# New order tables for a gated recurrent-attention and GeGLU kernel, and an earlier load of its guard flag

## The chip, the cores and the metric

One NeuronCore of a Trainium2 chip runs the kernel alone. Five engines work side by side: TensorE (PE, matmuls; the loading of its weights is shown as PEld), VectorE (DVE), ScalarE (ACT), GpSimd (POOL) and SyncE (SP), which here issues nearly all transfers. Each has its own queue of instructions and works through it in order; semaphores tie the queues together. The metric is the device time of one execution in microseconds.

## The reference

The input `x` (2048 x 448) is layer-normed. One branch is a recurrent attention in four segments of 512 positions with 16 heads of 28: causal softmax attention inside each segment, mixed with a read from a memory that the earlier segments have written. The other branch is a GeGLU feed-forward net of width 1792. The result is `x + s * silu(ffn)`.

```python
for s in range(N):                       # N = 4 segments
    logits = einsum(qs, ks) * scale + mask
    a_dot = softmax(logits) @ vs
    pq = phi(qs)                         # phi(t) = t + 1 if t > 0 else exp(t)
    a_mem = (pq @ M) / (pq @ z + 1e-06)
    o = g * a_mem + (1 - g) * a_dot      # g = sigmoid(beta)
    pk = phi(ks)
    M = M + pk^T @ vs
    z = z + sum(pk)
...
xn = layernorm(x)
s = attention(xn) @ wo
g = silu((gelu(xn @ w_gate) * (xn @ w_up)) @ w_down)
return x + s * g
```

## The kernel before

`fast_path` computes everything with all weights held in SBUF. It takes the softmax without a running maximum, which is allowed as long as the logits stay small. `guard` works out from the weights' norms whether they do, and leaves a 0 or 1 in the one-element tile `oki`. At the end every engine loads that flag into a register (`load_ok`, L1264) and branches on it (`tc.If`, L1679): with 1 the program is over, with 0 the slow `general_path` is run after it. The branch jumps over the code of `general_path`.

The work is cut into some 1170 named operations, each an `Op` with the engines that may run it, its length and latency, what it depends on, and which buffers it takes or uses. For segment `s`:

- `sc{s}{k}` are the ten steps of scores (L984), `ex{s}{k}{0,1}` their exponentials on ACT (L999, 128 x 1024 each), `mk` the causal masks on POOL (L1010), `pv` the products with the values (L1046), `ou` the copy of the sums out of PSUM (L882).
- `wq`, `wk`, `wv{s}{n}` are the projections (L713; two `full` units of three matmuls, then a `visit` `wr...` with the two half-height ones), `ev...` their evictions, `tq`, `tk`, `tr` DMA transposes on SP.
- `exwk`, `exwq` (L825), `mi` (L830) and `ph` (L838, L843) make phi; `up` (L859) adds to the memory, `rd{s}{g}` on PE (L897) reads it; `den`, `dc`, `rd{s}{side}{j}` and `rb` are transfers that invert and broadcast the denominators, `sm` and `ca` (L908, L952) multiply by them, and `cb` (L955) sums both sides into the single buffer `oT`.
- `gu` and `gh` (L1088, L1103) are the gate and up projections, `ge` the gelu on ACT (L1113), `hm` the product on DVE (L1118); `dn{s}{b}{k}` is the down projection of a block of 128 rows in groups of up to five matmuls (L1148), `th` and `sg` its silu, `wo{s}{b}` the output projection (L1173), `fm` and `fa` (L1178, L1164) the closing product and sum, `st` the store. The last block (L1192 to L1222, `last_block`) is cut into three column pieces `330`, `331`, `332`; the last store, `st332`, is issued by ACT, all others by SP.

`arrange` puts all operations into one list. It keeps a clock for each engine, counts for each operation the length and latency written at its definition, and takes, of what could start soonest (within `AHEAD`), the operation with the lowest `prio`. `PRIO` overrides the priority of each operation by name; `STEP` says behind which step of the scores a piece of PE work, or a phi of segment 2, may come. The list that comes out is then issued in this order, and each engine's queue keeps it. So the lengths and the tables shape the program that is built, and nothing else: at run time the engines go by their queues and semaphores.

The four stages of feed-forward and attention follow one another as `ORDER` says: G0, A0, A1, G1, A2, G2, A3, G3, and the last down projections. In A0 to A3 the PE fills the time between score steps with projections of the next segments, down projections and memory reads. Scores of the first two segments go through three pairs of PSUM banks, those of the others through two. The loads of `wo_sb` (four pieces), of `x_sb` for segments 2 and 3 and of the two halves of `wd_sb` are issued by SP among the transposes towards the end of G0; the first `dn` group of a block reads only the first half of `wd_sb`.

Of the kernel before, what the change touches and what calls it, by code (L numbers as in the profile page):

```python
# [53 lines left out]
class Buf:  # L54
# [284 lines left out]
def fast_path(tc, A_x, A_wq, A_wk, A_wv, A_wo, A_beta, B_w_gate, B_w_up, B_w_down, out):  # L339
# [19 lines left out]
    with ExitStack() as ctx:  # L359
# [89 lines left out]
        def act(name, n, fn, func=None, **kw):  # L449
            return op(name, {"ACT": (n / 1200 + 0.05, n / 1200 + 0.165)}, fn, act=func, **kw)  # L450

        def dve(name, t, fn, **kw):
            return op(name, {"DVE": (t, t + 0.085)}, fn, **kw)
# [1259 lines left out]
```

## Time and profile before

| | |
|---|---|
| median of 3 runs | 231.68 us (231.41 to 234.36) |
| the profiled execution | 232.09 us |
| its span, first to last instruction | 230.3 us |
| granted TensorE clock, mean | 0.996 |
| DMA over the span | 25.12 MB, mean 109 GB/s |

The profile is of one execution. Its times are counted from the span's start; what lies around the span is 1.8 us. A row of the windows gives a stretch, its length, then for PE, PEld, DVE, ACT and POOL the busy time and the number of instructions, then the granted PE clock (1.00 is full), the mean busy share of the DMA engines and the GB/s that they moved. A row of the timeline gives the start, the length, the engine, the line, the operation with its tiles, and in brackets how long the engine had been idle before and what released it. Rows of one line (L1264, L1679) give the shortest, median and longest duration in ns, and the first and last start. An engine with a q behind its name (ACTq, SPq) stands for its sequencer: transfers issued, loads of registers, branches, semaphores.

### The profile page before, as it was taken

How to read it: one execution, taken by the hardware profiler on the slowest of the kernel's cores; microseconds unless marked ns; L12 is line 12 of the kernel's file. 1: busy time of each engine (PE TensorE's matmuls, PEld its weight loads, DVE VectorE, ACT ScalarE, POOL GpSimd, SP SyncE). 2: the span in 40 equal slices, each digit the busy share in tenths (PEclk: the TensorE clock that was granted, in tenths of full speed). 3: DMA queues.
4: the chain of work that ended last, by engine and by line, in shares of the span. 5: the costliest groups of instructions: out<-in, count | busy, mean ns of one | idle time of the engine just before them, and what ended most of it. 6: DMA issues, size and time to landing. Idle time of an engine off the chain costs nothing.

```text
span 230.3 us, 4484 instructions
## 1 busy us (share of the span) xinstructions
PE 220.0 (96%) x1571; PEld 96.0 (42%) x1571; DVE 153.7 (67%) x291; ACT 152.0 (66%) x211; POOL 129.4 (56%) x222
## 2 busy tenths in 40 slices
PE   7999999889999999999999999999999999999980
PEld 3544443333544434344444444444444434444560
DVE  3799998868955795773865686873646445457381
ACT  4799636999898779333788879433788874323120
POOL 8501400679488699504599989671198488406200
PEclk9999999999999999999999999999999999999998
DMA  7999369954336882317702232273400037152011
GB/s 213 274 364 223 70 149 252 248 113 90 32 76 72 201 99 59 89 43 194 184 25 65 41 76 65 55 191 89 93 1 6 10 83 188 39 142 55 5 58 31
DMA packets 44710, 25.12 MB, mean 109 GB/s; under 512 B 30808, under 2 KB 40856, under 8 KB 44680
## 3 DMA queue, kind: packets, MB, share of 16 engines
q1 hardware_dynamic: 43704, 24.05, 45.8%
q10 hardware_dynamic: 976, 0.71, 1.0%
q8 instruction: 14, 0.23, 0.4%
q14 instruction: 16, 0.13, 0.2%
HBM read 16.00 MB, written 2.98 MB: 82 GB/s over the span
## 4 chain that ended last, share of the span: by engine, by line
PE 74%; ACT 8%; DVE 6%; DMA 5%; issue 2%; SPq 1%; ACTq 0%; DVEq 0%
PE pp L1088 13%; PE ps L1088 13%; PE ps L1148 13%; PE ps L713 10%; ACT pt L999 6%; PE ps L1173 4%; PE pp L984 4%; PE ps L1046 3%; PE pp L1103 3%; PE ps L1103 3%; DMA rb<-rdr 2%; PE ps L571 2%; DMA rdr<-dc 2%; DMA qT<-e 2%; PE pp L1148 2%
## 5 line engine op out<-in xcount | busy, mean ns | idle before, releaser
L999 ACT ACTIVATE pt<-pp 128x1024 bf16<-128x1024 f32 x75 | 73.3, 1037 | 12.2 <-PE pp L984 10.2
L1010 POOL TENSOR_SCALAR_AFFINE_SELECT pt<-pt 128x256 bf16<-128x256 bf16 x128 | 53.8, 444 | 26.0 <-ACT pt L999 23.4
L1148 PE MATMUL ps<-wd_sb,hT 128*128 128x448 bf16 x182 | 39.2, 354 | 0.5 <-DVE qs L749 0.4
L1113 ACT ACTIVATE gl<-pp 128x512 bf16<-128x512 f32 x28 | 15.8, 595 | 29.1 <-PE pp L1103 23.3
L1148 PEld LDWEIGHTS <-hT 128*128 128x128 bf16 x210 | 18.8, 98 | 20.6 <-issue 5.5
L1118 DVE TENSOR_TENSOR hT<-gl,pp 128x512 bf16<-128x512 bf16 x28 | 18.4, 681 | 11.5 <-ACT gl L1113 11.5
L1118 DVE TENSOR_TENSOR hT<-gl,ps 128x512 bf16<-128x512 bf16 x28 | 18.7, 677 | 10.9 <-ACT gl L1113 8.4
L1113 ACT ACTIVATE gl<-ps 128x512 bf16<-128x512 f32 x28 | 16.6, 597 | 13.1 <-PE ps L1088 6.7
L1088 PEld LDWEIGHTS <-wu_sb 128*128 128x128 bf16 x168 | 16.4, 98 | 20.0 <-issue 0.3
L1088 PEld LDWEIGHTS <-wg_sb 128*128 128x128 bf16 x168 | 14.9, 98 | 22.5 <-issue 7.2
L908 POOL TENSOR_TENSOR om<-om,rb 128x512 f32<-128x512 f32 x12 | 14.9, 1269 | 16.2 <-DMA rb<-rdr 16.2
L713 PEld LDWEIGHTS <-xnT 128*128 128x128 bf16 (+1 forms) x192 | 15.0, 97 | 20.6 <-issue 10.1
L1088 PE MATMUL ps<-xnT,wg_sb 128*128 128x512 bf16 x84 | 22.8, 380 | 0.0
L955 POOL TENSOR_TENSOR oT<-oa,om 128x512 bf16<-128x512 f32 x12 | 15.9, 1334 | 12.3 <-DVE oa L952 12.3
L1088 PE MATMUL pp<-xnT,wg_sb 128*128 128x512 bf16 x84 | 22.8, 380 | 0.0
L1088 PE MATMUL ps<-xnT,wu_sb 128*128 128x512 bf16 x84 | 22.7, 379 | 0.1
L1088 PE MATMUL pp<-xnT,wu_sb 128*128 128x512 bf16 x84 | 22.7, 379 | 0.0
L1164 POOL TENSOR_TENSOR oo<-sg,x_sb 128x448 bf16<-128x448 f32 (+1 forms) x13 | 12.9, 995 | 12.7 <-DVE sg L1215 10.1
L984 PE MATMUL pp<-qT,kT 32*128 32x512 bf16 (+3 forms) x238 | 17.3, 301 | 1.9 <-ACT pt L999 1.8
L830 POOL TENSOR_SCALAR e<-e 128x896 bf16<-128x896 bf16 (+1 forms) x12 | 12.8, 1068 | 10.9 <-ACT e L825 10.9
L645 POOL TENSOR_TENSOR rs<-rs,nhalf 128x1 f32<-128x1 f32 (+1 forms) x7 | 6.1, 883 | 16.5 <-DVE rs L640 16.5
L882 DVE COPY oa<-ps 128x512 f32<-128x512 f32 x16 | 10.9, 683 | 5.8 <-PE ps L1046 5.5
(119 smaller groups left out, 327.1 us busy)
## 6 DMA issues: line engine op xcount, KB each, us to landing
rb<-rdr SPq DMA_DIRECT2D x28, 256.0 KB
out_dram<-oo SPq DMA_DIRECT2D x15, 112.0 KB
wd_sb<-in_B_w_down_dram SPq DMA_DIRECT2D x2, 784.0 KB
x_sb<-in_A_x_dram SPq DMA_DIRECT2D x3, 448.0 KB
rdr<-dc SPq DMA_DIRECT2D x28, 32.0 KB
wg_sb<-in_B_w_gate_dram SPq DMA_DIRECT2D x2, 384.0 KB
wu_sb<-in_B_w_up_dram SPq DMA_DIRECT2D x2, 384.0 KB
wg_sb<-in_B_w_gate_dram SPq DMA_DIRECT2D x1, 576.0 KB
```

Source lines behind the costliest of these rows:

```text
L713: nc.tensor.matmul(out=self.bank.ap()[:, 0:D], lhsT=self.xT.ap()[r, c, n * P:(n + 1) * P], rhs=self.w[r, c, :], **kw)
L908: oU[s, g, 1] = t, gps(f"sm{s}{g}", 1.22, lambda t=t, r=r: nc.gpsimd.tensor_tensor(out=t.ap(), in0=t.ap(), in1=r.ap(), op=ALU.mult), deps= ...
L955: oT[s][1].append(gps(f"cb{s}{g}", 1.22, lambda g=g, t=t, tm=tm: nc.gpsimd.tensor_tensor(out=dst.ap()[:, g, :], in0=t.ap(), in1=tm.ap(), o ...
L984: nc.tensor.matmul(out=S2[i // 2].ap(i % 2)[:, c0:c0 + n], lhsT=kT[s][0].ap()[r, g, kb * P:(kb + 1) * P], rhs=qT[s][0].ap()[r, g, kb * P:L ...
L999: nc.scalar.activation(out=dst, in_=src, func=ACT.Exp, scale=scale)
L1010: nc.gpsimd.affine_select(out=v, in_=v, pattern=[[0, 2], [1, P]], compare_op=ALU.is_ge, fill=0.0, base=0, channel_multiplier=-1)
L1088: nc.tensor.matmul(out=bf[fc].ap(i), lhsT=w[:, c, fc * P:(fc + 1) * P], rhs=xT.ap()[:, c, :], start=begins and c == 0, stop=not begins and ...
L1103: nc.tensor.matmul(out=bf[fc].ap(i), lhsT=wh_sb[r, fc * P:(fc + 1) * P], rhs=xT.ap()[r, NC3, :], start=fc in begins, stop=fc in ends)
L1113: a = act(f"ge{s}{fc}", L, lambda: nc.scalar.activation(out=gl.ap(), in_=bf[fc].ap(0), func=ACT.Gelu_apprx_tanh), func="gelu", deps=[o], a ...
L1118: nc.vector.tensor_tensor(out=hT[s][0].ap()[:, fc, :], in0=gl.ap(), in1=bf[fc].ap(1), op=ALU.mult), deps=[a] + held,
L1148: nc.tensor.matmul(out=bank.ap()[:, 0:D], lhsT=hT[s][0].ap()[:, fc, b * P:(b + 1) * P], rhs=wd_sb[:, fc, :], start=(fc == 0), stop=(fc == ...
L1164: o = op(f"fa{s}{b}{h}", eng, lambda: (nc.vector if o.on == "DVE" else nc.gpsimd).tensor_tensor(out=oo.ap()[:, r], in0=t.ap()[:, r], in1=x ...
```

## The change

All entries of `PRIO` and most of `STEP` have new values; the operations that they order are the same. Five lengths at the operations' definitions are changed: the latency of an ACT and of a DVE operation, the power on POOL in the layer norm (`pw`), phi of the queries on DVE, and the exponentials of the scores. The flag's load is issued as soon as `th332` and `m332`, the last tanh and the last product of the closing block, have been issued, in place of after everything; and its value's bounds check is left out.

```diff
 PRIO = {
-    "ag00": -1122.63, "ag01": -1135.403, "ag10": -834.064, "ag11": -1044.988, "ag12": -837.494,
...
+    "ag00": -89.052, "ag01": -89.062, "ag10": -262.926, "ag11": -262.956, "ag12": -89.072,
...
 }
 STEP = {
-    "dn000": 9, "dn0010": 10, "dn005": 2, "dn010": 3, "dn0110": 7, "dn015": 6, "dn020": 3,
...
+    "dn000": 10, "dn0010": 3, "dn005": 6, "dn010": 0, "dn0110": 4, "dn015": 2, "dn020": 1,
...
 }
@@
         def act(name, n, fn, func=None, **kw):
-            return op(name, {"ACT": (n / 1200 + 0.05, n / 1200 + 0.165)}, fn, act=func, **kw)
+            return op(name, {"ACT": (n / 1200 + 0.05, n / 1200 + 0.18)}, fn, act=func, **kw)
 
         def dve(name, t, fn, **kw):
-            return op(name, {"DVE": (t, t + 0.085)}, fn, **kw)
+            return op(name, {"DVE": (t, t + 0.09)}, fn, **kw)
@@
-                o = gps(f"pw{s}{bs[0]}", 0.56, lambda r=r: nc.gpsimd.tensor_tensor(
+                o = gps(f"pw{s}{bs[0]}", 0.61, lambda r=r: nc.gpsimd.tensor_tensor(
@@
-                pqT[s][1].append(dve(f"ph{nm}{s}{half}", 1.47, lambda:
+                pqT[s][1].append(dve(f"ph{nm}{s}{half}", 1.35, lambda:
@@
-                    x = act(f"ex{s}{k}{pr}", 2 * L, ex, func="exp", deps=[o],
+                    x = act(f"ex{s}{k}{pr}", 2 * L + 24, ex, func="exp", deps=[o],
@@
         def load_ok():
-            got["ok"] = nc.values_load(oki[0:1, 0:1], min_val=0, max_val=1)
+            got["ok"] = nc.values_load(oki[0:1, 0:1], min_val=0, max_val=1,
+                                       skip_runtime_bounds_check_because="it is the least of comparisons")
@@
         with tc.manual_schedule():
+            closing = {f"th{LAST}{NB - 1}2", f"m{LAST}{NB - 1}2"}
             for o in arrange(ops):
                 if o.fn is not None:
                     o.fn()
-            load_ok()
+                closing.discard(o.name)
+                if not closing and "ok" not in got:
+                    load_ok()
```

The two programs have the same number of instructions on PE and DVE. The orders that they give each engine, where the prediction goes into them, read as follows (score steps marked with ^, visits with ~):

```
PE, start of A0, before: sc00^ wk10 wk11 wr1wk0~ wk13 wk12 wr1wk2~ sc01^ sc02^ wq11 wq10 wr1wq0~ sc03^ dn010 sc04^
PE, start of A0, after:  sc00^ wk10 wk11 wr1wk0~ sc01^ wq10 dn010 wq11 wr1wq0~ sc02^ dn015 sc03^ wv10 dn0110 wv11 wr1wv0~ sc04^
SP, before: tr10 tr13 wo_in0 x2 tr11 tr12 wo_in3 wd_in0 wo_in2 wo_in1 x3 wd_in1
SP, after:  tr10 tr13 wo_in0 wo_in3 wo_in2 wo_in1 x2 tr11 tr12 wd_in1 wd_in0 x3
ACT, A0, before: ex011 ex020 ex021 ... ex051 exwk10 ex060 ex061 exwk11 ex070 ... ex081 exwq11 ex090 ex091 exwq10 ex100
ACT, A0, after:  ex011 exwk10 ex020 ex021 ... ex090 ex091 exwk11 ex100 ex101 exwq10 ex110 ex111 exwq11
DVE, end of G2, before: hm212 ca21 hm213 ca22 ca20 ca23 evwv30 evwv31
DVE, end of G2, after:  hm212 hm213 ca20 ca21 fm11 evwv30 evwv31
PE, start of A3, after: sc30^ dn210 wo11 dn230 dn235 sc31^ dn2310 wv30 wv31 wr3wv0~
PE, end, before: dn3010 dn325 dn3210 wo33 wo32 dn330a dn335a dn3310a dn330b ... dn3310c
PE, end, after:  dn330a dn300 ... dn305 dn3010 wo30 wo33 dn335a dn3310a dn330b ... dn3310c
DVE, end, before: m330 y330 fa330 m331 y331 m332 y332 fa332 load
DVE, end, after:  m330 y330 m331 y331 m332 load y332 fa332   (fa330 on POOL)
ACT, end, before: th332 st332 load branch
ACT, end, after:  th332 load st332 branch
SP, end, before: st330 st331 load check branch
SP, end, after:  st330 load st331 branch
```

356 rows, old and new, of tables (PRIO, STEP) are left out of this document.

## The prediction

> **What bounds the kernel now.** I read the page first (busy shares, the slices, the chain of waits), then the windows, one stretch per stage, then the timeline of the two places where TensorE (PE) stands, and last the lines of the closing branch.
>
> ```profile
> PE 220.0 (96%) x1571; PEld 96.0 (42%) x1571; DVE 153.7 (67%) x291; ACT 152.0 (66%) x211; POOL 129.4 (56%) x222
> PE   7999999889999999999999999999999999999980
> PE 74%; ACT 8%; DVE 6%; DMA 5%; issue 2%; SPq 1%; ACTq 0%; DVEq 0%
> ```
>
> PE is at work in 220.0 of the span's 230.3 us, and 74% of the chain that ended last is PE. The other engines are each busy about two thirds of the time, so they matter only where one of them makes PE wait. The windows say where that is (first column the stretch, then its length and PE's busy time in it; DVE, ACT and POOL follow).
>
> ```profile
> 1.26:16.40 15.14, 15.01 (x91) 7.21 (x93) 10.82 (x32) 11.79 (x26) 7.46 (x27) 1.00 1.01 302
> 16.40:39.00 22.60, 22.54 (x120) 8.93 (x114) 21.18 (x51) 14.95 (x25) 3.66 (x3) 1.00 0.84 177
> 39.00:52.00 13.00, 11.15 (x94) 4.54 (x90) 9.61 (x25) 12.46 (x17) 8.04 (x19) 1.00 0.94 185
> 52.00:64.00 12.00, 11.88 (x120) 5.31 (x120) 10.73 (x18) 10.90 (x14) 8.37 (x17) 1.00 0.40 59
> 64.00:140.00 76.00, 76.00 (x602) 32.75 (x600) 51.29 (x82) 56.27 (x71) 56.56 (x91) 1.00 0.44 93
> 140.00:162.00 22.00, 22.00 (x126) 9.07 (x124) 13.75 (x21) 10.74 (x17) 12.47 (x12) 1.00 0.41 112
> 162.00:187.00 25.00, 24.55 (x204) 10.30 (x204) 15.12 (x26) 20.72 (x24) 16.95 (x33) 1.00 0.10 23
> 187.00:217.80 30.80, 30.76 (x176) 13.52 (x176) 15.07 (x25) 11.69 (x18) 14.80 (x16) 1.00 0.35 90
> 217.80:225.60 7.80, 6.08 (x60) 4.38 (x58) 5.88 (x15) 2.51 (x6) 0.49 (x1) 1.00 0.16 52
> 225.60:230.30 4.70, 0.00 (x0) 0.00 (x0) 0.00 (x0) 0.00 (x0) 0.00 (x0) 0.79 0.12 29
> ```
>
> Between 1.26 and 217.8 PE is idle for 0.13 + 0.06 + 1.85 + 0.12 + 0.00 + 0.00 + 0.45 + 0.04 = 2.65 us, and 1.85 of that is the start of the first attention (39 to 52), where ACT is busy 12.46 of 13.00. The end has 1.72 us more (217.8 to 225.6) and 4.70 us with no work on any engine. Both programs hold the same instructions on PE, so a new order can save PE time only out of these idle stretches. That caps what can be won: 2.65 us in the middle, plus what the closing part gives. 2% of 231.68 is 4.6 us, about what a measurement of this kernel can tell from no change.
>
> **The tail: the guard's load.** The rows are the load of `oki` (L1264) on three engines, the branch that tests it and what follows it (L1679), and the last instructions.
>
> ```profile
> L1264 DVEq TENSOR_LOAD <-oki x1: 541/541/541, 225.3 to 225.3; - x1
> L1264 ACTq TENSOR_LOAD <-oki x1: 479/479/479, 226.0 to 226.0; - x1
> L1679 DVEq COMPARE_BRANCH  x1: 72/72/72, 226.0 to 226.0; - x1
> L1679 ACTq COMPARE_BRANCH  x1: 58/58/58, 226.6 to 226.6; - x1
> L1679 DVEq EVENT_SEMAPHORE  x1: 21/21/21, 228.9 to 228.9; - x1
> L1679 ACTq EVENT_SEMAPHORE  x1: 17/17/17, 229.3 to 229.3; - x1
> 224.47 0.25 DVE L1212 TENSOR_TENSOR sg<-sg,ps 128x96 f32<-128x96 f32 x1
> 224.75 0.25 ACT L1209 ACTIVATE th<-ps 128x96 f32<-128x96 f32 x1 [1.12 <-DVE sg L1212]
> 225.03 0.26 DVE L1215 SCALAR_TENSOR_TENSOR sg<-th,sg 128x96 f32<-128x96 f32 x1 [0.32 <-ACT th L1209]
> 225.33 0.26 DVE L1164 TENSOR_TENSOR oo<-sg,x_sb 128x96 bf16<-128x96 f32 x1
> 225.62 0.37 ACTq L1222 DMA_DIRECT2D out_dram<-oo  x1
> ```
>
> ACT issues the last store at 225.62, 0.37 long; then it loads `oki` (226.0, 0.48), branches at 226.6, and its next instruction starts at 229.3: 2.7 us behind the branch. DVE branches at 226.0 and goes on at 228.9, 2.9 us behind. ACT is last, and only the final handshakes stand behind it until 230.3. In the new program order ACT's load lies between the last tanh (`th332`) and the store, so 0.48 us goes from in front of ACT's branch: it branches at 226.1 and goes on at 228.8. DVE must not be later than that: its load now stands between `m332` (224.47) and `y332` (225.03), so its branch comes right behind `fa332`, at 225.4, and it goes on at 228.3. That gives **-0.5 us**.
>
> The load is moved past instructions on three queues. On ACT it runs from about 224.8 to 225.3 while ACT would wait for `fa332` (over at 225.59): hidden; without that cover it costs 0.48 us. On DVE it takes 0.54 us between the starts 224.47 and 225.03, 0.56 us apart, in which DVE waits for ACT's tanh anyway. In the old place it began with `fa332` (225.3), not behind its end (225.59), so I count it as hidden; if it had to wait for the end of `m332` (224.72), `y332` would start 0.23 us late, with `fa332` and the last store behind it. On SP it now stands ahead of the second last store, and the bounds check behind it is gone; SP ends by waiting for the others, so I count nothing. On PE and POOL its place does not change. Its wait is for DVE's result of the guard, written long before. Bounds of this term: -0.55 and +0.2.
>
> The Trainium skill, "DMA: Bandwidth & Descriptors", section "Latency and other measured facts", puts the floor of such a register load at about 600 ns; by it this term would be about -0.6 instead of -0.5. The rows here (479 to 541 ns) are shorter, and the rows decide.
>
> **The new tables: the first attention.**
>
> ```profile
> 39.21 3.14 PE L713 MATMUL ps<-wk_sb,xnT 128*128 128x448 bf16 x16
> 43.79 0.39 PE L984 MATMUL pp<-qT,kT 32*128 32x256 bf16 x6 [1.01 <-ACT pt L999]
> 44.12 1.60 PE L713 MATMUL ps<-wq_sb,xnT 128*128 128x448 bf16 x8
> 46.43 1.11 PE L1148 MATMUL ps<-wd_sb,hT 128*128 128x448 bf16 x5 [0.36 <-DVE qs L749]
> 49.41 0.39 PE L984 MATMUL pp<-qT,kT 32*128 32x512 bf16 x2 [0.48 <-ACT pt L999]
> 40.25 1.94 ACT L999 ACTIVATE pt<-pp 128x1024 bf16<-128x1024 f32 x2
> 42.71 1.02 ACT L999 ACTIVATE pt<-pp 128x1024 bf16<-128x1024 f32 x1 [0.53 <-PE ps L984]
> 51.92 1.08 ACT L825 ACTIVATE e<-kn 128x896 bf16<-128x896 bf16 x1
> ```
>
> PE's 1.85 us of idle here are the three waits 1.01, 0.36 and 0.48, two of them for ACT's exponentials. The old order puts two pairs of projections (16 matmuls, 3.14 us) behind the first scores `sc00`; so the second scores `sc01` come at 42.3, ACT has nothing to do for 0.53 us, and then PE has nothing between `sc01` and `sc02` and waits 1.01. The new order is `sc00`, one pair (8 matmuls, about 1.5), `sc01`, then `wq10`, `dn010`, `wq11` and the visit, `sc02`, `dn015`, `sc03`. Worked out: `sc00` ends at 39.2, the pair at 40.75; half of `sc01` needs the banks of the first exponential, which ends at 40.25 + 1.94/2 = 41.2, so PE idles 0.5; `sc01` is over at 41.6 and `wq10` (three of eight matmuls, 0.6) at 42.2. The second pair of exponentials then starts without ACT's 0.53. Next is `dn010`, which reads the first half of `wd_sb`, and that is the question.
>
> ```profile
> 34.77 0.38 SPq L563 DMA_DIRECT2D wd_sb<-in_B_w_down_dram  x1
> 36.65 0.59 SPq L563 DMA_DIRECT2D wd_sb<-in_B_w_down_dram  x1
> 33.00:44.50 11.50, 10.49 (x69) 4.09 (x68) 9.43 (x25) 7.29 (x10) 2.54 (x5) 1.00 1.28 277
> 44.50:46.00 1.50, 1.50 (x11) 0.52 (x9) 1.43 (x4) 1.50 (x3) 1.14 (x4) 1.00 0.40 90
> ```
>
> In the old order the half that `dn010` reads is issued first (34.77), the other half last (36.65), and the loads run at 277 GB/s until about 44.5. In the new order SP issues the four pieces of `wo_sb`, then `x_sb` for segment 2, two transposes, the second half of `wd_sb`, the first half, and `x_sb` for segment 3 (448 KB) last. If the total still ends at 44.5, the first half ends 448 KB / 277 GB/s = 1.6 us before, at 42.9: `dn010` waits 0.7 us. Bounds: none, if SP's row of issues starts earlier; and 46.43 - 42.2 = 4.2, since the old program's first reader started only then. I take 0.7, by the rate. The idle here becomes 0.5 + 0.7 = 1.2 instead of 1.85. Three of ACT's segment-1 phi exponentials (about 1.0 each, the last row of ACT) also leave this stage for the next, where ACT has room (56.27 of 76.00 busy). I take **-0.6**, with -1.97 (all idle of 39 to 64) and +2.85 (0.5 + 4.2 - 1.85) as ends.
>
> **The rest of the tables.** The start is dealt out anew (memsets on POOL, evictions between ACT and DVE, ACT's early exponential behind the first evictions); PE's idle there is 0.13 us, its chain of transposes and evictions is the same: -0.2, between -0.5 and +0.5. From 52 us on the idle to be won is 0.12 + 0.45 + 0.04 = 0.6 us; every gap it closes may be opened elsewhere, since the buffers and the scores' order stay as they are: 0, between -0.6 and +3. At the end one addition (`fa330`, below) goes from DVE to POOL, which takes 0.36 us off DVE's closing row, but five matmuls of 192 columns come before the last full block instead of behind it (0.4 us at the pair's rate), so that DVE gets that block later: 0.
>
> ```profile
> 223.60 0.36 DVE L1164 TENSOR_TENSOR oo<-sg,x_sb 128x192 bf16<-128x192 f32 x1
> ```
>
> **Sum.** -0.5 - 0.6 - 0.2 + 0 = -1.3 us. The profiled execution took 232.09 (span 230.3 and 1.8 around it), 0.4 above the median of the runs, 231.68. So 230.8 for a like execution, and **230.4 us** as the median; chance 0.42.
>
> **Rivals.**
> - *Only the tail counts.* The gaps of the middle move instead of closing; PE shows 76.00 of 76.00 busy over the long middle, so there is nothing to win there. 231.68 - 0.5 = 231.2. Chance 0.20.
> - *All idle goes.* If `wd_sb` is there in time and the starting stalls close: -0.5 - 1.97 - 0.6 = -3.1, 228.6. Against it: half of `sc01` has to wait for the first exponential. Chance 0.14.
> - *Slower: `dn010` stands before its weights.* PE works in order, so `wq11`, `sc02` and through them ACT stand behind `dn010`. Past 42.2 each microsecond that the first half of `wd_sb` lands later costs one; against my sum the whole breaks even at 44.2, and at 46.43 it is -0.5 + 2.85 = +2.3, 234.0. For it: the load is now behind its twin. Against: the rate above. Chance 0.15.
> - *Slower by more: a queue order that holds a bank.* Behind the third up-projection stage DVE multiplies by the broadcast reciprocals before it empties projection banks:
>
> ```profile
> 164.85 2.06 DVE L952 TENSOR_TENSOR oa<-oa,rb 128x512 f32<-128x512 f32 x3
> 166.84 1.14 DVE L749 CAST vaug<-ps 128x448 bf16<-128x448 f32 x2
> L571 PE MATMUL ps<-oT x9: 607/634/634, 1.3 to 4.7; 128*128 128x512 bf16 x9
> ```
>
>   In the new order `ca20`, `ca21` and `fm11` (which now waits for `wo11`) precede these casts, and one side's broadcasts wait for the other side's reciprocal. If the broadcasts land 5 us later, PE's next projections lack a bank; the three pieces put before them (`wo11`, `dn230`, `dn235`) cover most of it. 2 to 4 us, 234 to 236. Chance 0.06.
> - *A cold clock.* If PE stood 3.4 us or more, it could restart at half rate, as the nine warming matmuls (from 1.3 to 5.3 us, 4.0 in all, where the eight somewhat narrower ones of the pair above take 1.60) show: 4.2 of idle and 2 more, 236 by the sum above. The granted clock was 1.00 through the wait of 1.01, so short waits do not do it. Chance 0.03. The Trainium skill, "TensorE: Matmul & The Clock Gate", Part 1, gives such a window of about 3.4 us after which an idle array falls to half clock; no run here shows it in mid-kernel.
>
> Range: 228.3 (near all idle gone) to 234.0 (the weights' upper bound), with about 0.2 outside. Chances: faster by over 2% (under 227.1) would take more than the idle that there is: 0.04. Slower by over 2% (over 236.3) needs the last two rivals at their ends or a stall not seen here: 0.07. Within: 0.89.
>
> **What would show it.** The last `oki` load on ACT ahead of its store, its branch at once behind the store and still some 2.7 us to the next instruction; the span's end about 4.2 instead of 4.7 us behind the last store's issue. In the first attention `sc02` behind five matmuls of L1148, with a PE wait for the DMA of `wd_sb` under 1.4 us, and no 1.01 for ACT. PE's idle from 1.26 to 217 near 2. I am wrong if a single PE wait of over 1.5 us appears anywhere, or if the idle behind the last store does not shrink.

## The result, and the profile after

The changed kernel takes 233.02 us (median of 14 runs, 231.92 to 234.49) against 232.10 for the kernel before (14 runs, 231.41 to 236.29). The ratio, here and below, is of the fast executions alone and not the quotient of the two medians (1.0040). It is 1.0049, 95% interval 1.0026 to 1.0072: slightly slower, by some 1.1 us, where 1.3 us faster was forecast. The same program again (e5 below) gave 1.0068 (1.0042 to 1.0095). The profiled execution took 232.26, a span of 230.5.

Four intervals say where the time went. The first ends with the start of the last gate or up matmul, the second with that of the last matmul at all, the third with the issue of the last store, the fourth with the span. The rows they come from, before and after: the last ones of a line's form (first and last start at the end of the counts), the last store, the span.

```profile
L1088 PE MATMUL ps<-xnT,wu_sb x84: 376/379/379, 20.0 to 209.8; 128*128 128x512 bf16 x84
L1204 PE MATMUL ps<-wd_sb,hT x42: 206/233/246, 221.0 to 223.7; 128*128 128x192 bf16 x14, 128*128 128x160 bf16 x14, 128*128 128x96 bf16 x14
```

```profile
L1084 PE MATMUL ps<-xnT,wu_sb x84: 379/379/379, 20.1 to 210.2; 128*128 128x512 bf16 x84
L1200 PE MATMUL ps<-wd_sb,hT x28: 206/219/233, 223.2 to 224.7; 128*128 128x160 bf16 x14, 128*128 128x96 bf16 x14
226.51 0.37 ACTq L1218 DMA_DIRECT2D out_dram<-oo  x1
core 0: 230.5 us, clock 0.999
```

The first grew from 209.8 to 210.2, the second from 13.9 to 14.5 (the traces' hundredths: 13.86 and 14.51), the third shrank from 1.95 (223.67 to 225.62) to 1.77, the fourth from 4.7 to 4.0. The tail did what was forecast; the program lost more ahead of it. The windows of the changed kernel (stretch, length, then busy time of PE, PEld, DVE, ACT, POOL):

```profile
39.00:52.00 13.00, 11.74 (x94) 4.71 (x91) 11.11 (x26) 12.16 (x15) 8.24 (x17) 1.00 0.61 153
52.00:64.00 12.00, 11.23 (x118) 5.14 (x117) 8.55 (x19) 11.35 (x16) 9.43 (x21) 1.00 0.38 73
140.00:162.00 22.00, 21.53 (x122) 8.90 (x121) 12.48 (x21) 10.61 (x16) 9.98 (x11) 1.00 0.28 81
187.00:217.80 30.80, 30.14 (x175) 13.25 (x173) 16.94 (x25) 11.98 (x19) 14.22 (x16) 1.00 0.35 92
```

The page's first line has PE at work as long as before (220.0) and DVE 4.0 us longer (153.7).

```profile
PE 219.9 (95%) x1571; PEld 95.8 (42%) x1571; DVE 157.7 (68%) x291; ACT 152.0 (66%) x210; POOL 128.2 (56%) x223
```

PE's idle from 39 to 52 fell from 1.85 to 1.26, but 0.77, 0.47 and 0.66 stand in stretches that had 0.12, 0.00 and 0.04, so that from 39 to 64 it did not fall (1.97, now 2.03). From 1.26 to 217.8 it rose from 2.65 to 3.83: the start (1.26 to 16.40) has 0.67 instead of 0.13, and the stretch from 162 to 187 has none instead of 0.45. Between 39 and 52 DVE is busy 11.11 of the 13 us where it was 9.61. The list of waits (total, number, longest) names whom PE waits for now:

```profile
PE ps L980 <- DVE kn L745: 1.3, 1, 1.3
PE pp L1084 <- DVE hT L1114: 0.5, 1, 0.5
PE ps L855 <- DVE vaug L745: 0.4, 1, 0.4
PE ps L1042 <- DVE e L745: 0.4, 1, 0.4
PE pp L1200 <- DVE hT L1114: 0.3, 1, 0.3
```

Before, the first attention waited for ACT's exponentials (1.01 and 0.48); now ACT is waited for once, for 0.3, and nearly all is DVE. The timeline shows what DVE does there, before and after, with the first gate matmul of G1 and the scaling of the last denominators (`dc`):

```profile
35.06 1.68 DVE L627 BATCH_NORM_STATS2 st<-x_sb 128x6 f32<-128x448 bf16 x3 [0.82 <-DMA x_sb<-in_A_x_dram]
40.85 1.15 DVE L749 CAST kn<-ps 128x448 bf16<-128x448 f32 x2 [0.69 <-PE ps L713]
89.55 0.82 PE L1088 MATMUL ps<-xnT,wg_sb 128*128 128x512 bf16 x3
198.11 0.25 DVE L919 TENSOR_SCALAR dc<-dc,igate 128x64 f32<-128x64 f32 x1 [0.93 <-DMA dc<-den]
206.66 0.69 DVE L952 TENSOR_TENSOR oa<-oa,rb 128x512 f32<-128x512 f32 x1 [1.93 <-DMA rb<-rdr]
```

```profile
35.17 2.21 DVE L623 BATCH_NORM_STATS2 st<-x_sb 128x6 f32<-128x448 bf16 x4 [0.99 <-DMA x_sb<-in_A_x_dram]
40.82 0.33 PE L980 MATMUL ps<-qT,kT 32*128 32x384 bf16 x1
40.95 0.88 DVE L648 TENSOR_SCALAR xn<-x_sb,mv,rs 128x448 bf16<-128x448 bf16 x2 [0.54 <-POOL rs L641]
41.75 1.14 DVE L745 CAST kn<-ps 128x448 bf16<-128x448 f32 x2
42.41 0.32 PE L980 MATMUL ps<-qT,kT 32*128 32x384 bf16 x1 [1.25 <-DVE kn L745]
89.99 0.82 PE L1084 MATMUL ps<-xnT,wg_sb 128*128 128x512 bf16 x3
200.48 1.23 DVE L915 TENSOR_SCALAR dc<-dc,igate 128x64 f32<-128x64 f32 x1 [1.58 <-DMA dc<-den]
209.57 0.69 DVE L948 TENSOR_TENSOR oa<-oa,rb 128x512 f32<-128x512 f32 x1 [4.42 <-DMA rb<-rdr]
210.18 1.27 DVE L1114 TENSOR_TENSOR hT<-gl,pp 128x512 bf16<-128x512 bf16 x2
```

Twice DVE stands for a transfer with work behind it in its queue that PE needs. Near 35 us four statistics of segment 2 wait 0.99 for `x_sb`; the products `hm010` to `hm013` come behind them, the normalizations `xn20` and `xn22` after those, and only then (41.75) the evictions `evwk10` and `evwk11`. The first of them frees the second bank of a pair that `sc01` needs: one matmul of `sc01` runs at 40.82, the next at 42.41. In the kernel before DVE stood 0.82 for the same load, which landed no sooner; but it had only three of the statistics ahead of the products and no normalization ahead of the evictions (40.85), and `sc01` came eight matmuls later, so PE did not wait.

Near 209 us `ca30` waits 4.42 for a broadcast, with `hm311`, `hm310` and `hm312` behind it, and the first down projections of the end need these. The old order has `ca30` ahead of `hm311` and `hm310` too; there it waited 1.93 and was through at 207.35. What the new order changed is the landing, 2.9 us later. The other side's denominators went out at 188.2 instead of 179.9, so its four broadcasts (256 KB each) are still being issued around the transfer `dc` of this side; from its issue to DVE's start that took 3.5 us (196.99 to 200.48) instead of 1.8 (196.30 to 198.11). That these broadcasts held it up is not tested.

### The profile page after: what moved, and what is told of

It reads as the page before. It is cut to its first block, busy times and chain, and to the rows that moved or that the text cites. A ratio compares the mean times of both kernels' runs of the same rounds, so it can differ in the third digit from the quotient of the medians.

```text
span 230.5 us, 4489 instructions
## 1 busy us (share of the span) xinstructions
PE 219.9 (95%) x1571; PEld 95.8 (42%) x1571; DVE 157.7 (68%) x291; ACT 152.0 (66%) x210; POOL 128.2 (56%) x223
## 5 line engine op out<-in xcount | busy, mean ns | idle before, releaser
L1144 PE MATMUL ps<-wd_sb,hT 128*128 128x448 bf16 x196 | 41.0, 353 | 0.0
L1144 PEld LDWEIGHTS <-hT 128*128 128x128 bf16 x210 | 19.3, 98 | 19.6 <-issue 3.4
L709 PEld LDWEIGHTS <-xnT 128*128 128x128 bf16 (+1 forms) x192 | 14.5, 96 | 20.7 <-issue 11.4
L641 POOL TENSOR_TENSOR rs<-rs,nhalf 128x1 f32<-128x1 f32 (+1 forms) x7 | 5.4, 771 | 23.4 <-DVE rs L636 23.4
L1160 POOL TENSOR_TENSOR oo<-sg,x_sb 128x448 bf16<-128x448 f32 (+2 forms) x14 | 13.4, 960 | 7.4 <-DVE sg L1211 7.4
L826 POOL TENSOR_SCALAR e<-e 128x896 bf16<-128x896 bf16 (+1 forms) x12 | 11.8, 987 | 5.5 <-ACT e L821 5.3
```

Source lines behind the costliest of these rows:

```text
L709: nc.tensor.matmul(out=self.bank.ap()[:, 0:D], lhsT=self.xT.ap()[r, c, n * P:(n + 1) * P], rhs=self.w[r, c, :], **kw)
L826: o = gps(f"mi{nm}{s}{half}", n / 1024, lambda: nc.gpsimd.tensor_scalar(out=t(), in0=t(), scalar1=1.0, scalar2=0.0, op0=ALU.min, op1=ALU.max),
L1144: nc.tensor.matmul(out=bank.ap()[:, 0:D], lhsT=hT[s][0].ap()[:, fc, b * P:(b + 1) * P], rhs=wd_sb[:, fc, :], start=(fc == 0), stop=(fc == ...
L1160: o = op(f"fa{s}{b}{h}", eng, lambda: (nc.vector if o.on == "DVE" else nc.gpsimd).tensor_tensor(out=oo.ap()[:, r], in0=t.ap()[:, r], in1=x ...
```

## The experiments

From e3 on the programs are written from a list: order, engine and banks of each operation as the planner gave them in one of the two kernels, and the named steps moved. e3 and e4 load the flag at the end, as before; from e5 on it is loaded early, as in the changed kernel. Each ratio is to the kernel before, run beside it; 6 or 12 runs each. The four intervals are from one profiled execution each, by the same rows as above (the last one to within 0.05, as the span is given in tenths):

| | ratio (95%) | to last gate/up | to last matmul | to store | to end |
|---|---|---|---|---|---|
| before | 1 | 209.81 | 13.86 | 1.95 | 4.68 |
| changed | 1.0049 (1.0026 to 1.0072) | 210.23 | 14.51 | 1.77 | 3.99 |
| e1 load only | 0.9974 (0.9945 to 1.0002) | 209.59 | 13.86 | 1.95 | 4.40 |
| e2 tables only | 1.0115 (1.0067 to 1.0164) | 212.01 | 14.66 | 1.78 | 4.94 |
| e3 new start | 1.0114 (1.0083 to 1.0144) | 210.75 | 13.86 | 1.94 | 4.65 |
| e4 new to A3 | 1.0074 (1.0047 to 1.0102) | 210.79 | 13.86 | 1.95 | 4.60 |
| e5 changed again | 1.0068 (1.0042 to 1.0095) | 210.23 | 14.75 | 1.77 | 4.25 |
| e6 evict first | 1.0043 (1.0020 to 1.0066) | 210.28 | 14.76 | 1.78 | 4.18 |
| e7 products first | 1.0024 (0.9999 to 1.0049) | 210.66 | 14.87 | 1.78 | 4.10 |
| e8 early x_sb | 1.0001 (0.9975 to 1.0027) | 208.98 | 14.65 | 1.78 | 4.09 |
| e9 e8 + dn330a | 1.0040 (1.0012 to 1.0068) | 210.13 | 15.10 | 1.78 | 4.08 |
| e10 e8 + evictions | 0.9997 (0.9973 to 1.0021) | 209.16 | 14.64 | 1.78 | 4.11 |
| e11 e8 + both | 1.0004 (0.9983 to 1.0026) | 211.07 | 15.12 | 1.78 | 4.13 |
| e12 old tables, load, early x_sb | 0.9973 (0.9953 to 0.9994) | 209.53 | 13.86 | 1.95 | 4.16 |
| e13 ca30 later | 1.0022 (0.9994 to 1.0049) | 209.52 | 13.86 | 1.77 | 4.14 |
| e14 DVE's order | 1.0032 (1.0005 to 1.0059) | 211.09 | 13.86 | 1.77 | 4.37 |
| e15 e14, old end | 1.0088 (1.0062 to 1.0113) | 211.72 | 13.86 | 1.94 | 4.08 |
| e16 early x_sb + ca30 | 0.9974 (0.9952 to 0.9997) | 210.31 | 13.86 | 1.78 | 4.14 |
| e17 norm later | 1.0120 (1.0074 to 1.0166) | 212.42 | 13.86 | 1.78 | 4.14 |
| e18 e16 + evictions | 0.9959 (0.9940 to 0.9978) | 208.89 | 13.86 | 1.78 | 4.07 |

### The load alone, the tables alone

```diff
 e1: the kernel before, with
+            closing = {f"th{LAST}{NB - 1}2", f"m{LAST}{NB - 1}2"}
             for o in arrange(ops):
...
-            load_ok()
+                closing.discard(o.name)
+                if not closing and "ok" not in got:
+                    load_ok()
 e2: the changed kernel without these lines
```

> The kernel before with the flag's load moved and its bounds check left out, tables and lengths as before. Theory (the tail gives what was forecast, the tables lose more): 0.5 us faster, ratio 0.998, and 4.0 to 4.2 us from the last store's issue to the span's end instead of 4.7. Rival (the load disturbs the closing chain and gives its gain back): ratio 1.000 with the last store 0.3 to 0.5 us later.

> The changed kernel with the flag's load put back at the end, with its check. Theory: the tables alone cost what the whole change cost and what the load gave besides, 1.1 + 0.5 = 1.6 us, ratio 1.007. Rival (the tables are neutral, and the early load is what makes the change slower): ratio 0.999 to 1.001.

e1: 0.9974, its tail 4.40. Over all profiles the tail is 4.60 to 4.94 where the load stands at the end (four of them) and 3.99 to 4.40 where it is early (the other sixteen), about 0.6 us. e2: 1.0115, so the tables alone lose; its profile also shows how far the loss can go in one execution. The load of `x_sb` was issued 1.3 us later in it than in the changed kernel's profile (first row: changed; then e2), behind a start of loads that ran later, and DVE stood 2.46 us (two of its six executions also had a lower mean clock, see the last section):

```profile
31.17 0.40 SPq L556 DMA_DIRECT2D x_sb<-in_A_x_dram  x1
```

```profile
32.44 0.40 SPq L556 DMA_DIRECT2D x_sb<-in_A_x_dram  x1
36.44 2.21 DVE L623 BATCH_NORM_STATS2 st<-x_sb 128x6 f32<-128x448 bf16 x4 [2.46 <-DMA x_sb<-in_A_x_dram]
PE pp L980 <- DVE hT L1114: 1.3, 2, 0.9
```

The last row is new: here even `sc00` waited for the products.

### Parts of the new order

```diff
 e3: one list of all operations
-before ...................................................
+changed, up to sc00 | before ..............................
 e4
+changed, up to sc30                        | before .......
```

> The new order up to the first scores sc00 (about 39 us), the old order from there, load at the end. Theory (many small waits, most of them behind the start, since sc00 starts at the same time in both profiles): within 0.3 us of the kernel before, ratio 0.999 to 1.001. Rival (the start makes the loss, through the evictions that run beside POOL's memsets): ratio 1.003 to 1.007.

> The new order up to sc30 (about 162 us), the old order from there, load at the end. Theory: the loss is about half made by then (sc30 came 0.3 us later in the profile of the changed kernel, the last store 0.9): ratio 1.001 to 1.003. Rival (it is the closing stage alone): ratio 1.000. Rival (it is all made in the first attention): ratio 1.006 or more.

e3 does not test the start: where the two lists meet, `sc01` got two pairs of banks instead of three, and PE waited for ACT to empty them:

```profile
PE pp L980 <- ACT pt L995: 2.7, 4, 2.0
```

Its 1.0114 is therefore not the start's; a part of it is the clock's (last section). `sc00` began at 38.52 in it (38.88 before, 38.72 after), so the profile shows no loss there. e4, with the new order up to A3 and the old end, is at 1.0074 with a closing stretch of 13.86: the number of the rival that puts the loss in the first attention, not the half that the theory had. But its two lists meet as well, at `sc30`. From the first gate matmul of G2 to that of G3 its profile has 49.1 us (139.90 to 188.99), and so has that of e15, with the same seam; the other runs with the new tables there have 47.8 to 48.7, those with the old 47.4 to 47.7. So a part of the 1.0074 is the seam's, and e4 does not say how much the first attention lost. That there is a loss behind it, the 14.5 to 14.8 of the closing stretch in the other runs say.

### The first attention

```diff
 DVE, changed:
 hm09 bn22 bn21 bn23 bn20 ag20 hm011 ag22 ag21 hm010 hm012 ag23 ep20 hm013 xn20 xn22 evwk10 evwk11 xn21 xn23
 e6:
-xn20 xn22 evwk10 evwk11
+evwk10 evwk11 xn20 xn22
 e7: e6, and
-hm09 bn22 bn21 bn23 bn20 ag20 hm011 ag22 ag21 hm010 hm012 ag23 ep20 hm013
+hm09 hm011 hm010 bn22 bn21 hm012 bn23 bn20 ag20 ag22 ag21 ag23 ep20 hm013
 e8, SP:
-wo_in0 wo_in3 wo_in2 wo_in1 x2 tr11
+x2 wo_in0 wo_in3 wo_in2 wo_in1 tr11
```

> The changed kernel once more, instruction for instruction: a second look at the spread of its times (231.9 to 234.5). Theory (the row of transfers on SP sets the spread: the load of x_sb for segment 2 lands between 35 and 36.4 us, and four of DVE's statistics wait for it ahead of the products of the feed-forward stage): the profile shows a DVE wait for x_sb of 0.6 to 2.5 us near 35 us, the longer the later sc00 starts and the longer the execution. Rival (the spread comes from the closing stage): sc00 at 38.7 whatever the time. Median ratio 1.004 to 1.006 either way.

> The changed kernel with the evictions evwk10 and evwk11 ahead of the two normalizations xn20 and xn22 on DVE. Theory (sc01 waits for its third pair of banks, and they for DVE): PE's wait of 1.25 us in front of sc01's second half shrinks to under 0.5, ACT's idle of 0.68 behind it goes: 0.5 to 0.9 us faster than the changed kernel, ratio to the kernel before 1.001 to 1.003. Rival (ACT bounds this stage, the wait only moves to another place): 1.004 to 1.006 as without the edit.

> The same, and besides DVE's products hm010 and hm011 ahead of all four statistics of segment 2, hm012 ahead of two. Theory (a late x_sb delays the products, which free the first scores' banks): sc00 no longer depends on the landing of x_sb; median 1.0 to 1.5 us below the changed kernel, ratio to the kernel before 0.998 to 1.001, and a narrower spread. Rival (the products were not late enough to matter): the same as the run with the evictions alone.

> The changed kernel with the load of x_sb for segment 2 ahead of the four pieces of wo_sb on SP instead of behind them, nothing else. Theory: x_sb lands about 1.9 us sooner, DVE's wait for it (0.99 in the profile) goes, hm010 comes 0.5 to 1 us sooner and with it the first evictions: 0.3 to 0.9 us faster than the changed kernel, ratio to the kernel before 1.001 to 1.004. Rival: 1.004 to 1.006, as without the edit.

e5, the changed kernel again: DVE stood 1.53 us for `x_sb`, `sc00` began at 38.52, and the closing stretch was longer too (14.75), so the landing is not the only source of the spread. e6: PE's wait for `kn` fell as expected, but the ratio only to 1.0043, within the interval of e5. e7: 1.0024; the products no longer wait, but now the evictions stand behind the statistics, and `evwq11` behind `bn30`, which stands for segment 3's `x_sb`. The waits of e6, and then of e7:

```profile
PE ps L980 <- DVE kn L745: 0.4, 1, 0.4
```

```profile
PE ps L980 <- DVE kn L745: 1.2, 1, 1.2
PE ps L980 <- DVE e L745: 0.8, 1, 0.8
```

e8, which moves no work at all, only one transfer ahead of four others, gained most: 1.0001. Its rows:

```profile
33.80 2.20 DVE L623 BATCH_NORM_STATS2 st<-x_sb 128x6 f32<-128x448 bf16 x4
41.06 0.32 PE L980 MATMUL ps<-qT,kT 32*128 32x384 bf16 x1 [0.45 <-DVE kn L745]
```

DVE does not stand for this load any more, and the second matmul of `sc01` runs at 41.06 instead of 42.41; the last gate or up matmul is 1.25 us earlier. The early issue does not secure it: in the profiles of e9 and e11 (below), which issue at the same place, DVE still stood 1.15 and 1.46. That makes pairs of one order with two landings: from `sc00` to the first gate matmul of G1, e8 took 51.01 us and e9 51.76, e10 50.89 and e11 51.65.

### More edits on top, and the old tables with the early load

```diff
 e9: e8, and PE
-dn330a dn300 dn320 ... wo30 wo33 dn335a
+dn300 dn320 ... wo30 wo33 dn330a dn335a
 e10: e8 and e6, and DVE
-bn30 evwq10 evwq11
+evwq10 evwq11 bn30
 e11: e9 and e10
 e12: the kernel before and e1, and SP
-wo_in0 x2 tr11
+x2 wo_in0 tr11
```

> The run with the early x_sb, and besides dn330a, five matmuls of the last block, back from the end of the last gate and up projections to where the old order has it, just ahead of dn335a. Theory (dn330a stands in front of the other down projections and waits for the products hm that DVE makes last, 0.3 to 0.8 us of PE's idle near 210 us): that wait goes, 0.3 to 0.7 us faster than with the early x_sb alone, ratio to the kernel before 0.997 to 0.999. Rival (DVE closes the kernel and the wait is absorbed behind it): no change, 0.999 to 1.001.

> The run with the early x_sb, and in the first attention DVE's evictions evwk10 and evwk11 ahead of xn20 and xn22, and evwq10 and evwq11 ahead of bn30, which waits for x_sb of segment 3. Theory: PE's two waits for evictions there (0.62 and 0.90 by the gaps between matmuls) go, and half of it or more reaches the end: 0.7 to 1.5 us faster than with the early x_sb alone, ratio to the kernel before 0.994 to 0.997. Rival (ACT's exponentials bound the stage, so only ACT's idle of it is won): 0.2 to 0.5 us, 0.998 to 0.999.

> Both of these edits on the run with the early x_sb. Theory: the gains add, 1.0 to 2.0 us below the early x_sb alone, ratio to the kernel before 0.991 to 0.996. Rival: no better than the better of the two.

> The kernel before with the early load of the flag, and the load of x_sb for segment 2 ahead of its first piece of wo_sb. Theory (the old order has sc01 behind 16 matmuls and the evictions ahead of the normalizations, so it does not depend on the landing): the early flag's load alone, ratio 0.996 to 0.999. Rival (every order gains by an early x_sb, the new tables are not special): ratio 0.992 to 0.995.

e9 went the other way: 1.0040, closing stretch 15.10. PE waits for the products whichever down projection comes first, and `dn330a` had covered a part of that:

```profile
209.66 0.69 DVE L948 TENSOR_TENSOR oa<-oa,rb 128x512 f32<-128x512 f32 x1 [4.60 <-DMA rb<-rdr]
211.59 1.11 PE L1144 MATMUL pp<-wd_sb,hT 128*128 128x448 bf16 x5 [1.08 <-DVE hT L1114]
```

So the cause stands on DVE, one step further back. e10 removed the longer wait for evictions that e8 still had in the first attention (0.7, behind `bn30`) and gained nothing by its ratio; e11 is no better. e12 gives the early flag's 0.9973 and no more. But in its profile DVE still stood 0.91 for the load, as long as before the edit (0.82), so e12 does not test whether the old order hangs on this landing.

### The end: ca30, and DVE's order as a whole

```diff
 e13: DVE
-ca30 hm311 hm310 hm312 ca31 hm313
+hm311 hm310 hm312 ca30 ca31 hm313
 e14: e13, and DVE
-hm09 bn22 bn21 bn23 bn20 ag20 hm011 ag22 ag21 hm010 hm012 ag23 ep20 hm013 xn20 xn22 evwk10 evwk11 xn21 xn23 du20 bn30 evwq10 evwq11
+hm09 hm011 hm010 hm012 bn22 bn21 hm013 bn23 evwk10 evwk11 bn20 ag20 ag22 ag21 ag23 ep20 xn20 xn22 xn21 xn23 du20 evwq10 evwq11 bn30
 e15: this, up to sc30 | before (without e13's edit)
```

> The changed kernel with one step moved on DVE: the multiplication ca30, which waits for a broadcast by transfer, behind the products hm311, hm310 and hm312 instead of ahead of them. Theory (DVE stands 4.4 us for the broadcast with these products behind it, and the down projections of the end wait for them): PE's wait near 210 us (0.47 to 0.83 in the runs with the new order) goes, the stretch from the last gate and up matmul to the last matmul falls from 14.5 to 14.9 towards 13.9 as in every run with the old end: 0.5 to 0.9 us faster than the changed kernel, ratio to the kernel before 1.001 to 1.004. Rival (what closes the kernel is DVE, and later multiplications delay the output projection as much): 1.005 to 1.007.

> The changed kernel with three things moved on DVE and nothing else: ca30 as in the run before; in front of the first attention all four products ahead of the four statistics of segment 2 or between them, and evwk10, evwk11 ahead of the normalizations; evwq10, evwq11 ahead of bn30. Theory (the loss is DVE standing in its queue for a transfer, with work behind it that PE needs): 1.0 to 2.0 us faster than the changed kernel, ratio to the kernel before 0.997 to 1.001, and sc01's wait under 0.7 us whenever x_sb lands. Rival (the first attention is bounded by ACT): no better than the run before.

> The new order up to sc30 with DVE's steps of the first attention moved as in the run before, the old order from sc30, the flag's load early. Theory: the stretch from the last gate and up matmul to the last matmul is 13.86 us as in all runs with the old end, and the first attention no longer loses: ratio to the kernel before 0.993 to 0.998, as fast as the old tables with the early load (0.997) or faster. Rival (the middle of the new order loses besides): 0.999 to 1.003.

e13 settles the end. The three products run before the broadcast is needed, and PE goes on without a stop (a group of three matmuls every 0.65 us, and `dn330a` in its turn at 209.74):

```profile
207.44 1.29 DVE L1114 TENSOR_TENSOR hT<-gl,pp 128x512 bf16<-128x512 bf16 x2 [3.00 <-ACT gl L1109]
208.72 0.69 DVE L1114 TENSOR_TENSOR hT<-gl,ps 128x512 bf16<-128x512 bf16 x1
209.32 1.28 DVE L948 TENSOR_TENSOR oa<-oa,rb 128x512 f32<-128x512 f32 x2
208.44 0.81 PE L1084 MATMUL ps<-xnT,wg_sb 128*128 128x512 bf16 x3
209.09 0.81 PE L1084 MATMUL ps<-xnT,wu_sb 128*128 128x512 bf16 x3
209.74 0.58 PE L1200 MATMUL pp<-wd_sb,hT 128*128 128x192 bf16 x5
```

The stretch is 13.86, as in every run with the old end, against 14.51 to 15.12 in all nine that have the new end with `ca30` ahead of the products. The ratio, 1.0022, is 0.3 to 0.5% below the two of the changed kernel, as expected; the intervals overlap, so it is the stretch that shows it. e14 and e15 refute my order for the first attention (e15's ratio holds the seam at `sc30` besides): `sc01`'s wait fell to 0.4, but `evwq11` now stood behind four normalizations, and PE waited 1.3 (e14) and 1.6 (e15) there.

```profile
PE ps L980 <- DVE e L745: 1.3, 1, 1.3
```

### Both edits together, and a last order of DVE

```diff
 e16: e8 and e13
 e17: e13, and DVE from e14's order
-ep20 xn20 xn22 xn21 xn23 du20 evwq10 evwq11 bn30
+ep20 evwq10 evwq11 xn20 xn22 xn21 xn23 du20 bn30
 e18: e10 and e13
```

> The changed kernel with the two single edits that helped: the load of x_sb for segment 2 ahead of the pieces of wo_sb, and ca30 behind three products. Theory (two separate places, each with DVE standing for a transfer ahead of work that PE needs): the gains add, 0.6 and 0.4% below the changed kernel, ratio to the kernel before 0.995 to 0.999, as fast as the old tables with the early load (0.997). Rival (one gain is absorbed by the other, or the gain of the early x_sb was chance): 1.000 to 1.003.

> The changed kernel with ca30 later, and on DVE the normalizations of segment 2 (xn20 to xn23, 1.6 us) and bn30 behind the evictions evwq10 and evwq11, the statistics between and behind the products; no transfer moved. Theory (what holds the first attention is that DVE does segment 2's normalization there four us earlier than the old order and stands for its load): PE's waits for evictions between 40 and 48 us sum to under 1.0 us, against 1.4 in the changed kernel and 2.1 in the run with three moves on DVE; ratio to the kernel before 0.996 to 1.000. Rival (DVE has too much to do there in any order, the wait goes to a later place): 1.001 to 1.004.

> The early x_sb, ca30 later, evwk10 and evwk11 ahead of xn20 and xn22, and evwq10, evwq11 ahead of bn30. Theory: 13.9 us from the last gate and up matmul to the last matmul, and the first attention as in the run with these edits before: ratio to the kernel before 0.994 to 0.998. Rival (the evictions were not what bounds, as that run's lack of a gain says): the same as with the early x_sb and ca30 alone, within 0.002.

e16: 0.9974, as forecast and as the old tables with the early load (0.9974): by the ratios, these two edits make good the whole loss. PE's waits of 0.4 for `vaug` and for `e` stay in it, as in e8 and e18, so they were not what the change lost. Its single profile is not the plainest witness, since DVE stood 2.61 us for `x_sb` of segment 3 in it (last gate or up matmul at 210.31). e17 refutes the idea that the early normalization is what is in the way: with it put later the waits between 40 and 48 us went, as expected, and a longer one came behind, since the eviction of `vaug` was late in its turn:

```profile
51.41 0.92 PE L1042 MATMUL ps<-pt,vaug 128*32 128x512 bf16 x16 [2.42 <-DVE vaug L745]
```

e18 is the fastest of all, 0.9959 (0.9940 to 0.9978), 0.4% below the kernel before; its interval overlaps those of e16 and of the old tables with the early load, so neither what the evictions add there nor a gain by the new tables is settled.

## Why the prediction was wrong

**The tail: right.** Forecast -0.5 us with 4.2 behind the last store; measured 4.0, and 0.6 us over the profiles. On DVE the load ran from 225.1 to 225.6, beside its last products and over before `y332` (225.93), and the last `oki` load is ACT's, with its next instruction still 2.7 us behind its branch:

```profile
L1260 ACTq TENSOR_LOAD <-oki x1: 581/581/581, 225.7 to 225.7; - x1
L1679 ACTq COMPARE_BRANCH  x1: 58/58/58, 226.9 to 226.9; - x1
L1679 ACTq EVENT_SEMAPHORE  x1: 17/17/17, 229.6 to 229.6; - x1
```

The load is 0.58 long here, closer to the floor of about 600 ns that the Trainium skill states ("DMA: Bandwidth & Descriptors", "Latency and other measured facts") than the 0.48 before.

**The first attention: the step that failed.** The sum took -0.6 from PE's idle there, by two questions: half of `sc01` against the banks of the first exponential (0.5 of wait), and `dn010` against `wd_sb` (0.7). `wd_sb` cost little: `dn010` did not wait in the changed kernel (43.32), nor in e8, where it came at 41.96; it waited 0.35 in e16 (until 42.89). So the slower rival built on it did not happen. `sc01` waited 1.25, but for the third pair of banks, which DVE empties. The prediction took DVE's evictions as done in time. It asked of SP's new row only who reads the last of its loads, not what stands on DVE behind the wait for `x2`; and it drew up DVE's order at the end of the kernel and of G2, but not here, where a fourth statistic came ahead of the products and two normalizations ahead of the evictions while PE's scores came earlier. So the demand for banks moved forward by eight matmuls and their supply back, by 0.9 us (40.85 to 41.75). The load itself was not later: SP issued it at 31.10 before and 31.17 after, and DVE's statistics began at 35.06 and 35.17.

How much this cost shows from the first matmul of `sc00` (38.88 before, 38.72 after) to the first gate matmul of G1, which have the same 448 matmuls between them in every run. With the old tables that took 50.67, 50.72 and 50.67 (before, e1, e12); with the new ones and no edit there 51.27, 52.04, 52.13, 51.35 and 51.41 (changed, e5, e2, e13, e4), in the mean 0.95 more, where 0.6 less had been forecast. Where DVE did not stand for `x_sb` of segment 2 (e8, e10, e18) it was still 51.01, 50.89 and 50.89. So 0.2 to 0.3 is lost by the order without any stand, and the stand adds to it (0.75 in e9 over e8, 0.76 in e11 over e10). No run with the new tables got through this stretch faster than the old ones.

**The rest: 0 forecast, 0.5 to 0.7 lost at the end.** From the first gate matmul of G1 to the last gate or up matmul the 0 was right: in the mean 120.0 us with the old tables and with the new. "Every gap it closes may be opened elsewhere" was the right worry without a place. The place was the closing stretch: +0.65 and +0.89 in the two profiles of the changed kernel, less 0.18 up to the last store, where POOL took over an addition. The prediction's sum for the end had that addition and PE's five matmuls in it, and no later broadcast. Its rival of a queue order in which DVE multiplies by broadcasts ahead of work for PE, because one side's broadcasts wait for the other side's reciprocal, had the mechanism, and was put at the end of G2, where the trace shows no such wait; at the end of G3 it happened, at a price of 0.65 to 0.89 instead of 2 to 4.

**The start** (-0.2): `sc00` came 0.16 earlier in the two profiles, right within what can be told.

**The sum.** First attention +0.95, closing stretch +0.8, up to the last store -0.2, start -0.2 and tail -0.6 make +0.8 us, 0.3% of 232; measured were 0.49 and 0.68%, so single profiles account for about half to two thirds of it and the rest stays open. The range (228.3 to 234.0) held the time, but the sign was wrong, and only offsetting terms (the tail's gain against losses that it had not named) kept the error small. The 2% that the prediction took for the least that can be told is too coarse: the intervals here are some 0.25% to either side. Its rival of all idle gone counts the 0.12 between 52 and 64 twice (in 1.97 and in 0.6); it comes to 228.7. The sentence "a single PE wait of over 1.5 us" would not have told: the largest is 1.25, and the loss lies in several of 0.3 to 1.3. PE's idle did not come near 2, which was the sign that failed. The wait of 0.5 near 150 us, where two phi of the queries (2.29 us) stand on DVE ahead of a product, came in some executions only; what it costs was not settled.

## What to carry to other kernels

For each instruction that waits for a transfer, list what stands behind it in its engine's queue, and who needs that: this, not the transfer's own readers alone, is what a late landing costs. Where work on PE moves forward, see that the engine that frees its banks does so too. And where a wait goes when one step is moved, look for the next in line before counting the gain: the orders with products and evictions put first (e14, e17) moved PE's stop to the next tile, while an earlier transfer and a later multiplication, which take the stop out of the queue, gained some 0.3 to 0.7% each.

## What the runs showed of the hardware

**A shorter stop than expected turned the clock down.** The prediction counted on 3.4 us of standing. In e17 PE stood 2.42 us, and the granted clock of the windows behind it (third column from the end) fell to 0.50:

```profile
51.40:52.00 0.60, 0.59 (x16) 0.41 (x16) 0.60 (x2) 0.00 (x0) 0.00 (x0) 0.84 0.53 106
52.00:53.00 1.00, 1.00 (x13) 0.28 (x3) 0.95 (x3) 0.00 (x0) 0.00 (x0) 0.50 0.62 126
55.00:56.00 1.00, 1.00 (x6) 0.32 (x4) 0.31 (x2) 1.00 (x2) 0.22 (x1) 0.89 0.64 129
```

It was 0.50 from 53 to 55 as well; by these shares half rate lasted from 51.8 to 55.2, some 3.4 us. A stop of 2.0 us, in e3, left it at 1.00:

```profile
43.00:46.00 3.00, 1.16 (x13) 0.58 (x13) 2.36 (x6) 2.52 (x3) 1.56 (x4) 1.00 0.60 94
```

The Trainium skill ("TensorE: Matmul & The Clock Gate", Part 1) has a free-running window of about 3.4 us, and half rate after at least one idle window. The length at half rate agrees with that window; but a stop of 2.42 us is shorter than one, so here the measurement decides, against the skill's condition and the prediction's 3.4.

The executions without a profile have only a mean clock. In e3 six of twelve have 0.983 to 0.989 and took 235.5 us in the mean; the other six have 0.993 to 0.995 and took 233.8. In e17 four of six have 0.982 to 0.989, in e2 two of six; the 29 executions of the kernel before beside e2 and e3 have 0.990 to 0.998. 3.4 us at half rate is 1.7 us of PE's work and 0.7% of the mean, which fits these differences. So by this estimate one and the same stop of 2 us or a little more turned the clock down in some executions and not in others; the stops of the unprofiled ones were not seen. It is a part of the ratios of e2, e3 and e17, and not of the changed kernel's loss: there one execution of 14 (0.986), and none of e5's six, is that low.

**One DVE instruction took four times as long beside POOL's memsets, in some executions.** The first centring of `x` took 1.46 us in the changed kernel's profile, and 0.34 in e5, the same program; PE's first transposes came 0.3 later for it. Of the 17 profiles with the new start, the eight in which it began between 3.87 and 4.10 us show 1.24 to 1.46, all with an end near 5.33; the nine in which it began earlier or later show 0.34 to 0.72.

```profile
3.87 1.46 DVE L658 TENSOR_SCALAR hT<-x_sb,mv 128x448 bf16<-128x448 bf16 x1
```

```profile
3.72 0.34 DVE L658 TENSOR_SCALAR hT<-x_sb,mv 128x448 bf16<-128x448 bf16 x1
```

The Trainium skill ("SBUF — State Buffer", "SBUF: two separate sides") describes a pair of ports that one of the two engines holds for a whole instruction; the long rows would fit that, and no run tested it.
